# Output projection in borrowed PSUM banks, the last Q products one step earlier, snapshots at high priority and phi of Q in pairs, in a linear-attention block with a ReGLU MLP

## The chip, the cores and the metric

The kernel runs on one core of a Trainium2 chip. The metric is the device time of one execution in microseconds (us), the median of several runs. A profile is one execution recorded by the hardware profiler; its span is somewhat shorter than that execution's own time.

## The reference

Input is x of 2048 tokens by 1024, in bf16. The block computes h = x + attention(layernorm(x)) and then h + MLP(layernorm(h)):

```python
qkv = (x @ wqkv) split into q, k, v of 32 heads with 32 columns each
phi = lambda t: jnp.where(t > 0, t + 1, jnp.exp(t)) + 1e-6
pq, pk = phi(q), phi(k)
kv = jnp.einsum("bhsd,bhse->bhde", pk, v)
z = jnp.einsum("bhsd->bhd", pk)
num = jnp.einsum("bhqd,bhde->bhqe", pq, kv)
den = jnp.einsum("bhqd,bhd->bhq", pq, z)[..., None] + 1e-6
o = (num / den) @ wo
...
gate = h_ln @ W_gate          # kept where positive, 0 elsewhere
up = h_ln @ W_up
out = h + (gate * up) @ W_down  # W_gate, W_up: 1024 x 3584
```

## The kernel before

**Large products.** They are done by a scheme of seven block products in place of eight (Strassen's, in Winograd's form) over two by two blocks; the sums of operands are made on VectorE. The generator `strassen` (L144) runs one unit: seven products for two neighbouring column tiles v = 0 and 1, in six phases, each ended by a `yield`. Its PSUM tiles come from the pool `pspool`: two banks of tag A, two of tag E, one of tag D. A collects products 1, 6, 7 and 4 one upon the other; after each of the first three a snapshot of A is copied to SBUF by ScalarE (`snap`, L149; the copy is L153). D takes product 2; E takes products 5 and 3. `fin` makes a result out of a PSUM tile and a snapshot.

**Stages.** First layernorm of x, K and V and the products kv and z, token tile by token tile (up to about 124 us in the profile). Then Q: `q_unit(s, c)` makes Q transposed for the half s of the columns of tokens, in units of two column blocks c and c + 1. The two units of s = 0 run alone (124 to 148 us). The two units of s = 1, twelve phases in all, are dealt out over eight attention steps (`QSTEPS` = 8) in the list `rest`: one or two phases behind each step. Each result of Q goes through phi: `phi_begin` (L189) adds the snapshot, and `phi_end` (L197) does an exp on ScalarE (L199), then a min with an add (L200) and a max (L201) on VectorE. Before the change that is done for each 128 x 512 tile by itself.

**Attention steps.** `attn_stages(t)` (L495) has five stages for a tile of 128 tokens: `nd` (numerators and denominators: eight matmuls L509 in three pieces, each a PSUM tile of tag "ab"; ScalarE takes Ln and Exp of the denominators, L513 and L515; VectorE multiplies, L516), `oT` (a DMA transpose, L523), `x_in` (a load of x, L527), `wo_h` (the output projection: two PSUM tiles "attn", also of tag "ab", with eight matmuls each, L536; VectorE adds x and sums rows, L538; the sum of both is scaled in L546; then on ScalarE the layernorm's Square, Ln, Exp, scale and normalise, L548 to L552) and `hn_T` (a DMA transpose of the normalised tile, L555). `attn_step(step)` issues stage k of the tile that began LAG[k] steps earlier, with LAG = (0, 1, 1, 2, 4), so in step n stand nd of tile n, oT and x_in of tile n - 1, wo_h of tile n - 2 and hn_T of tile n - 4. Behind hn_T of the later tiles of a half, `left_sums` makes the operand sums for the MLP (L117 to L120). The pool "ab" has three PSUM banks. Tiles 0 to 7 are those of s = 0, tiles 8 to 15 those of s = 1.

**What comes after.** From step 8 on, four "early quads" of the MLP (units of `strassen` with `early_quad`, matmuls L693, results L702 to L708, written to DRAM) run beside the steps: the first phase of the first quad is issued ahead of step 8, the others from step 12 on in the list `flow`. Then all PSUM pools are closed, the pool `accs` takes their banks (tag A two buffers of two banks, X and Y one each), and the rest of the MLP runs (`quad`, matmuls L773; then the down projection, L934 and L1105) in an order written out by hand for TensorE, ScalarE and VectorE.

**What sets the order.** In the part up to there the order of the instructions on each engine is planned when the kernel is built: a planner (Tile) takes the instructions in the order in which the program lists them, which is their priority, draws ready ones of a lower priority forward where an engine would stand idle by its own costs, and gives out the tiles of a tag as they come free. `tc.high_priority()` puts what is issued in it ahead of the others. A block ahead of everything else (L378) runs 16 matmuls on zeros ("spin", L383) while the first data load; their PSUM tile has tag E.

Of the kernel before, what the change touches and what calls it, by code (L numbers as in the profile page):

```python
# [31 lines left out]
def block_kernel(ctx: ExitStack, tc: tile.TileContext, x, wqkv, wo, wg, wu, wd, out, H: int):  # L32
# [111 lines left out]
    def strassen(pool, work, mm, fin, sbufs=3):  # L144


        A, E, snaps = {}, {}, {}

        def snap(v, nm):  # L149
            if v == 0:  # L150
                snaps[nm] = work.tile([P, 2, NW], FP32, tag="snap", bufs=sbufs, name=nm)
            snaps[nm, v] = snaps[nm][:, v, :]
            nc.scalar.copy(out=snaps[nm, v], in_=A[v][:])  # L153

        def m2(v):
            d = pool.tile([P, NW], FP32, tag="D", bufs=1, name="Dq")
            mm(d, 2, v, True)
            fin(0, 0, v, d, snaps["m1", v])

        for v in range(2):  # L160
            A[v] = pool.tile([P, NW], FP32, tag="A", bufs=2, name="Aq")
            mm(A[v], 1, v, True)
            snap(v, "m1")
        yield
        m2(0)
        for v in range(2):
            mm(A[v], 6, v, False)
            snap(v, "u2")
        m2(1)
        yield  # L170
        for v in range(2):
            E[v] = pool.tile([P, NW], FP32, tag="E", bufs=2, name="Eq")
            mm(E[v], 5, v, True)
        yield
        for v in range(2):
            mm(A[v], 7, v, False)
            snap(v, "u3")
            fin(1, 1, v, E[v], snaps["u3", v])
        yield
        for v in range(2):  # L180
            mm(A[v], 4, v, False)
            fin(1, 0, v, A[v], None)
        yield
        for v in range(2):
            mm(E[v], 3, v, False)
            fin(0, 1, v, E[v], snaps["u2", v])
        yield
# [9 lines left out]
    def phi_end(dst, e):  # L197

        nc.scalar.activation(out=e, in_=dst, func=ACT.Exp, bias=negb[:, 0:1], scale=1.0)  # L199
        nc.vector.tensor_scalar(out=e, in0=e, scalar1=1.0, scalar2=PHI_EPS, op0=ALU.min, op1=ALU.add)  # L200
        nc.vector.tensor_tensor(out=dst, in0=dst, in1=e, op=ALU.max)  # L201
# [9 lines left out]
    with ExitStack() as actx:  # L211
# [166 lines left out]
        with tc.high_priority():  # L378
            zero = asmall.tile([P, NW], BF16, tag="zero", bufs=1, name="zero")
            nc.vector.memset(zero[:], 0.0)  # L380
            spin = pspool.tile([P, NW], FP32, tag="E", bufs=2, name="spin")
            for n in range(SPIN):
                nc.tensor.matmul(spin[:], lhsT=zero[:, 0:P], rhs=zero[:], start=True, stop=True)  # L383
            ln_T(atiles[0])
# [45 lines left out]
    def q_unit(s, c):  # L430

        left = left_ops(xT[s], xS[s])
        ready = {}

        def mm(ps, m, v, start):
            for kc in range(KH):
                nc.tensor.matmul(ps[:], lhsT=rq[m - 1][:, kc, (c + v) * P:(c + v + 1) * P],  # L437
                                 rhs=left[m - 1][:, kc, :], start=(start and kc == 0),
                                 stop=(kc == KH - 1), skip_group_check=True)

        def fin(i, j, v, ps, m):
            dst = pqT[:, j * KH + c + v, i * HS + s * SW:i * HS + (s + 1) * SW]
            phi_begin(dst, ps, m)
            e = qw[-1].tile([P, NW], BF16, tag="e", name="e")
            phi_end(dst, e[:])

        return strassen(pspool, qw[-1], mm, fin)

# [46 lines left out]
    def attn_stages(t):  # L495

        i, r = divmod(t * P, HS)
        s, r = divmod(r, SW)
        st = {}

        def nd():
            o_sb = bwork.tile([P, D], BF16, tag="o_sb", name="o_sb")
            st["o"] = o_sb
            held.append(o_sb)
            ov = o_sb[:].rearrange("p (k h e) -> p k h e", k=KC, h=HPC)
            for c0, n in pieces:
                ps = ndpool.tile([P, NW], FP32, tag="ab", name="nd")
                for c in range(c0, c0 + n):
                    nc.tensor.matmul(ps[:, (c - c0) * NDW:(c - c0 + 1) * NDW], lhsT=pqT[:, c, t * P:(t + 1) * P],  # L509
                                     rhs=kvz[:, c, :], start=True, stop=True)  # L510
                ndv = ps[:, 0:n * NDW].rearrange("p (k w) -> p k w", w=NDW)
                den = bsmall.tile([P, GPB, HPC], FP32, tag="den", name="den")
                nc.scalar.activation(out=den[:, 0:n], in_=ndv[:, :, P:NDW], func=ACT.Ln, bias=deps[:], scale=1.0)  # L513
                rd = bsmall.tile([P, GPB, HPC], FP32, tag="rd", name="rd")
                nc.scalar.activation(out=rd[:, 0:n], in_=den[:, 0:n], func=ACT.Exp, scale=-1.0)  # L515
                nc.vector.tensor_tensor(  # L516
                    out=ov[:, c0:c0 + n], in0=ndv[:, :, 0:P].rearrange("p k (h e) -> p k h e", h=HPC),
                    in1=rd[:, 0:n, :].unsqueeze(3).to_broadcast([P, n, HPC, Dh]), op=ALU.mult)

        def oT():  # L520
            oT = bwork.tile([P, D], BF16, tag="oT", bufs=XB, name="oT")
            st["oT"] = oT[:].rearrange("p (c t) -> p c t", c=KC)
            nc.sync.dma_start_transpose(out=st["oT"], in_=st["o"][:])  # L523

        def x_in():
            x_sb = bwork.tile([P, D], BF16, tag="x_res", bufs=XB, name="x_res")
            nc.sync.dma_start(out=x_sb[:], in_=xf[t * P:(t + 1) * P, :])  # L527
            st["x"] = x_sb

        def wo_h():  # L530
            h_sb = st["x"]
            tot = bsmall.tile([P, 2], FP32, tag="tot", name="tot")
            for j in range(2):
                ps = abpool.tile([P, NW], FP32, tag="ab", name="attn")
                for c in range(KC):
                    nc.tensor.matmul(ps[:], lhsT=st["oT"][:, c, :], rhs=wo_sb[:, c, j * NW:(j + 1) * NW],  # L536
                                     start=(c == 0), stop=(c == KC - 1))
                nc.vector.scalar_tensor_tensor(out=h_sb[:, j * NW:(j + 1) * NW], in0=ps[:], scalar=1.0,  # L538
                                               in1=h_sb[:, j * NW:(j + 1) * NW], op0=ALU.mult, op1=ALU.add,
                                               accum_out=tot[:, j:j + 1])  # L540
            nc.sync.dma_start(out=h_dram[i][s][:, r // P, :], in_=h_sb[:])
            st["hn"] = bwork.tile([P, D], BF16, tag="hn", bufs=HB, name="hn")

            sm = bsmall.tile([P, 6], FP32, tag="sm", name="sm")
            nmean, var, lnv, rstd, nmr = (sm[:, i:i + 1] for i in range(5))
            nc.vector.tensor_scalar(out=nmean, in0=tot[:, 0:1], scalar1=tot[:, 1:2], scalar2=-1.0 / D,  # L546
                                    op0=ALU.add, op1=ALU.mult)
            nc.scalar.activation(out=st["hn"][:], in_=h_sb[:], func=ACT.Square, bias=nmean, scale=1.0, accum_out=var)  # L548
            nc.scalar.activation(out=lnv, in_=var, func=ACT.Ln, bias=LN_EPS, scale=1.0 / D)
            nc.scalar.activation(out=rstd, in_=lnv, func=ACT.Exp, scale=-0.5)  # L550
            nc.scalar.activation(out=nmr, in_=nmean, func=ACT.Identity, scale=rstd)
            nc.scalar.activation(out=st["hn"][:], in_=h_sb[:], func=ACT.Identity, bias=nmr, scale=rstd)  # L552

        def hn_T():
            nc.sync.dma_start_transpose(out=hnT[s][i][:, :, r:r + P], in_=st["hn"][:])  # L555

        return nd, oT, x_in, wo_h, hn_T
# [7 lines left out]
    def attn_step(step):  # L565
        for k in range(len(LAG)):
            n = step - LAG[k]
            if n in begin_at:
                n = begin_at.index(n)
                stages[n][k]()  # L570
                if k == len(LAG) - 1 and n % STS >= NT:
                    left_sums(hnT[n // STS], hns[n // STS], slice(n % NT * P, (n % NT + 1) * P), nc.vector)

    rest = [p for s in range(1, NS) for c in range(0, KH, 2) for p in [q_unit(s, c)] * 6]
    for step in range(QSTEPS):
        attn_step(step)
        if step:
            for _ in range(-(-len(early_loads) // (QSTEPS - step))):
                early_loads.pop(0)(held[step][0:1, 0:1])
        for p in rest[step * len(rest) // QSTEPS:(step + 1) * len(rest) // QSTEPS]:  # L580
            next(p)
    q1ctx.close()
    xctx[1].close()
# [748 lines left out]
```

## Time and profile before

| | us |
|---|---|
| median of 3 runs | 748.55 |
| lowest and highest | 747.36, 749.38 |
| the profiled execution, its own time | 748.8 |
| its span in the profile | 747.0 |
| TensorE busy in the span | 725.9 |
| VectorE, ScalarE busy | 568.4, 324.6 |
| projection of tile 6 starts (step 8) | 204.97 |
| first matmul of the hand-ordered MLP (L773) starts | 297.49 |

How to read the profile: PE is TensorE's matmuls, PEld its weight loads, DVE is VectorE, ACT is ScalarE, POOL is GpSimd, SP the queue that issues most DMAs. A group is named by its line in the kernel, then engine, operation, what it writes and what it reads. A wait "PE attn L536 <- DVE o_sb L516: 2.4, 4, 0.9" says that TensorE stood idle ahead of instructions of L536 until an instruction of L516 on VectorE was over: 2.4 us in total, 4 times, at most 0.9. In a table of stretches each line has the stretch, its length, the busy time of each engine with the number of its instructions, the granted clock, the DMA share and GB/s.

### The profile page before, as it was taken

The page shows a single profiled execution, that of the slowest core. Times are in us where ns is not written, and L with a number is a line of the kernel's source. Part 1 is how long each engine was busy: PE and PEld are TensorE (multiplying, and loading weights), DVE is VectorE, ACT ScalarE, POOL GpSimd, SP SyncE. Part 2 cuts the span into 40 slices and gives each one's busy share as a digit, 9 for nine tenths or more (in the row PEclk, how much of TensorE's full clock was granted, in tenths as well). Part 3 has the DMA queues.
Part 4 walks back from the last instruction along what each step waited for, and adds up shares of the span by engine and source line. Part 5 has one row for each costly group of instructions (what it writes and reads, how often), then busy time and mean ns, then how long its engine had stood idle before and what let it go on. Part 6 is the DMA issues. An engine that isn't in the chain of part 4 may idle for free.

```text
span 747.0 us, 10654 instructions
## 1 busy us (share of the span) xinstructions
PE 725.9 (97%) x4020; PEld 382.2 (51%) x4020; DVE 568.4 (76%) x1023; ACT 324.6 (43%) x596; POOL 5.8 (1%) x44
## 2 busy tenths in 40 slices
PE   7999999999889999999999999999999999999997
PEld 3444555444344444444444444444444458888666
DVE  6997644777886767678777788877787469996797
ACT  4876554778767645344444344343435220000000
POOL 0000000000000000000000000000000000000000
PEclk9999999999999999999999999999999999999999
DMA  9766002069777525164837349476574399988822
GB/s 317 159 145 154 1 1 94 20 146 249 170 173 172 134 79 183 39 182 121 237 127 207 125 140 317 149 211 212 183 261 149 101 388 361 317 284 299 306 79 79
DMA packets 146580, 132.03 MB, mean 177 GB/s; under 512 B 50913, under 2 KB 128097, under 8 KB 146529
## 3 DMA queue, kind: packets, MB, share of 16 engines
q1 hardware_dynamic: 135392, 123.23, 54.4%
q10 hardware_dynamic: 11136, 8.13, 3.4%
q8 instruction: 31, 0.51, 0.3%
q14 instruction: 21, 0.16, 0.1%
HBM read 79.95 MB, written 39.85 MB: 160 GB/s over the span
## 4 chain that ended last, share of the span: by engine, by line
PE 79%; DVE 8%; ACT 5%; DMA 5%; issue 1%; SPq 0%; POOL 0%; DVEq 0%; ACTq 0%
PE accA L773 22%; PE accY L773 8%; PE accX L773 8%; PE accA L1105 8%; PE attn L536 5%; PE Aq L297 3%; PE accA L934 3%; PE accX L1105 3%; PE Aq L437 3%; PE accY L1105 2%; DMA hn<-hn 2%; PE Aq L693 2%; PE Eq L297 2%; PE accX L934 2%; PE accY L934 2%
## 5 line engine op out<-in xcount | busy, mean ns | idle before, releaser
L783 ACT ACTIVATE gu<-gu 128x512 bf16<-128x512 bf16 x72 | 45.4, 630 | 131.9 <-DVE gu L782 127.4
L778 ACT COPY snap<-accA 128x1024 f32<-128x1024 f32 x72 | 72.4, 1008 | 37.0 <-PE accA L773 36.9
L536 PE MATMUL attn<-wo_mem,oT 128*128 128x512 bf16 x256 | 57.8, 379 | 3.4 <-DVE o_sb L516 3.1
L773 PEld LDWEIGHTS <-tg 128*128 128x128 f16 x384 | 37.6, 98 | 45.3
L773 PEld LDWEIGHTS <-tu 128*128 128x128 f16 x384 | 37.6, 98 | 45.3
L782 DVE TENSOR_TENSOR gu<-accY,snap 128x1024 bf16<-128x1024 f32 x36 | 43.9, 1219 | 9.7 <-ACT snap L778 9.7
L153 ACT COPY u<-Aq 128x512 f32<-128x512 f32 x56 | 32.2, 581 | 43.9 <-PE Aq L297 20.3
L782 DVE TENSOR_TENSOR gu<-accX,snap 128x1024 bf16<-128x1024 f32 x36 | 43.9, 1219 | 7.2 <-PE accX L773 4.7
L773 PE MATMUL accA<-hn,tg 128*128 128x512 f16 (+1 forms) x192 | 49.3, 379 | 0.0
L773 PE MATMUL accA<-hn,tu 128*128 128x512 f16 (+1 forms) x192 | 49.3, 379 | 0.0
L1105 PEld LDWEIGHTS <-x 128*128 128x128 f16 (+1 forms) x448 | 43.8, 98 | 5.5
L773 PEld LDWEIGHTS <-wg 128*128 128x128 bf16 x288 | 28.2, 98 | 34.9 <-issue 1.1
L773 PEld LDWEIGHTS <-wu 128*128 128x128 bf16 x288 | 28.2, 98 | 34.0
L536 PEld LDWEIGHTS <-oT 128*128 128x128 bf16 x256 | 25.0, 97 | 35.0 <-issue 6.7
L786 DVE TENSOR_TENSOR hq<-gu 128x512 bf16<-128x512 bf16 x48 | 20.3, 423 | 14.3 <-ACT gu L783 14.2
L297 PEld LDWEIGHTS <-xT 128*128 128x128 bf16 (+1 forms) x192 | 18.6, 98 | 24.5 <-issue 3.2
L516 DVE TENSOR_TENSOR o_sb<-nd,rd 128x384 bf16<-128x384 f32 (+1 forms) x48 | 22.8, 507 | 8.6 <-ACT rd L515 7.5
L1105 PEld LDWEIGHTS <-xs 128*128 128x128 f16 x280 | 27.4, 98 | 3.2
L538 DVE SCALAR_TENSOR_TENSOR x_res<-attn,x_res 128x512 bf16<-128x512 f32 x32 | 22.0, 688 | 6.3 <-PE attn L536 6.2
L934 PEld LDWEIGHTS <-x 128*128 128x128 bf16 (+1 forms) x168 | 16.5, 98 | 19.6
L1111 DVE TENSOR_TENSOR snap<-accA,u 128x1024 f32<-128x1024 f32 x16 | 19.5, 1220 | 8.3 <-PE accA L1105 8.1
L773 PE MATMUL accA<-hn,wg 128*128 128x512 bf16 x96 | 24.6, 379 | 0.8 <-DVE gu L702 0.8
(232 smaller groups left out, 1415.0 us busy)
## 6 DMA issues: line engine op xcount, KB each, us to landing
x<-x_dram SPq DMA_DIRECT2D x17, 896.0 KB, 8.2
x_dram<-hq SPq DMA_DIRECT2D x28, 512.0 KB, 3.0
wg<-in_B_W_gate_dram SPq DMA_DIRECT2D x14, 512.0 KB, 5.2
wu<-in_B_W_up_dram SPq DMA_DIRECT2D x14, 512.0 KB, 7.4
wraw<-in_B_W_down_dram SPq DMA_DIRECT2D x14, 512.0 KB, 4.9
x_dram<-hq SPq DMA_DIRECT2D x28, 256.0 KB, 2.6
t_dram<-wt SPq DMA_DIRECT2D x28, 256.0 KB, 2.2
xd<-x_dram SPq DMA_DIRECT2D x6, 896.0 KB, 7.2
```

The costliest lines, as they stand in the source:

```text
L153: nc.scalar.copy(out=snaps[nm, v], in_=A[v][:])
L297: nc.tensor.matmul(ps[:], lhsT=left[m - 1][:, kc, r + v * P:r + (v + 1) * P], rhs=right[m - 1][:, kc, :], start=(start and kc == 0), stop= ...
L437: nc.tensor.matmul(ps[:], lhsT=rq[m - 1][:, kc, (c + v) * P:(c + v + 1) * P], rhs=left[m - 1][:, kc, :], start=(start and kc == 0), stop=( ...
L516: nc.vector.tensor_tensor(out=ov[:, c0:c0 + n], in0=ndv[:, :, 0:P].rearrange("p k (h e) -> p k h e", h=HPC), in1=rd[:, 0:n, :].unsqueeze(3 ...
L536: nc.tensor.matmul(ps[:], lhsT=st["oT"][:, c, :], rhs=wo_sb[:, c, j * NW:(j + 1) * NW], start=(c == 0), stop=(c == KC - 1))
L538: nc.vector.scalar_tensor_tensor(out=h_sb[:, j * NW:(j + 1) * NW], in0=ps[:], scalar=1.0, in1=h_sb[:, j * NW:(j + 1) * NW], op0=ALU.mult, ...
L773: nc.tensor.matmul(ps[:, v, :], lhsT=w[v][n - 1][:, kc, :], rhs=left[n - 1][:, kc, :], start=(t is not None and kc == 0), stop=(kc == KH - ...
L778: nc.scalar.copy(out=st[nm][:], in_=halves(st["A"]))
L782: add(out=g[:], in0=halves(st[nm]), in1=st[base][:], op=ALU.add)
L783: nc.scalar.activation(out=g[:, 0, :], in_=g[:, 0, :], func=ACT.Relu)
L934: nc.tensor.matmul(ps[:, t * NW:(t + 1) * NW], lhsT=x_tile(n, s, kh)[:, f, (t0 + t) * P:(t0 + t + 1) * P], rhs=w_tile(n, kh)[:, f, :], sta ...
L1105: nc.tensor.matmul(pv[:, tt, :], lhsT=left(m)[:, f, tt * P:(tt + 1) * P], rhs=right(m)[:, f, :], start=(t is not None and f == 0 and tt % ...
```

## The change

Four edits that hang together, and one small one. The output projection `wo_h` takes its two PSUM tiles from tag E of `pspool` in steps 8 to 11, which are the projections of tiles 6 to 9, and from "ab" in all other steps. In step 7 the phases of Q that are due (the last two) are issued ahead of the attention step, not behind it. Every snapshot copy is issued at high priority. Phi of Q puts both column blocks of a unit into one tile: `phi_begin` stays as it was for each, and `phi_end` runs once for 128 x 2 x 512 when the second is there. The spin tile takes tag A.

```diff
@@ strassen, snap @@
             snaps[nm, v] = snaps[nm][:, v, :]
-            nc.scalar.copy(out=snaps[nm, v], in_=A[v][:])
+            with tc.high_priority():
+                nc.scalar.copy(out=snaps[nm, v], in_=A[v][:])
@@ at the start of the K and V stage @@
-            spin = pspool.tile([P, NW], FP32, tag="E", bufs=2, name="spin")
+            spin = pspool.tile([P, NW], FP32, tag="A", bufs=2, name="spin")
@@ q_unit @@
         def fin(i, j, v, ps, m):
-            dst = pqT[:, j * KH + c + v, i * HS + s * SW:i * HS + (s + 1) * SW]
-            phi_begin(dst, ps, m)
-            e = qw[-1].tile([P, NW], BF16, tag="e", name="e")
-            phi_end(dst, e[:])
+            pair = pqT[:, j * KH + c:j * KH + c + 2, i * HS + s * SW:i * HS + (s + 1) * SW]
+            phi_begin(pair[:, v], ps, m)
+            if v == 1:
+                e = qw[-1].tile([P, 2, NW], BF16, tag="e", name="e")
+                phi_end(pair, e[:])
@@ attn_stages @@
-        def wo_h():
+        def wo_h(borrow):
...
             for j in range(2):
-                ps = abpool.tile([P, NW], FP32, tag="ab", name="attn")
+                if borrow:
+                    ps = pspool.tile([P, NW], FP32, tag="E", bufs=2, name="attn")
+                else:
+                    ps = abpool.tile([P, NW], FP32, tag="ab", name="attn")
@@ attn_step @@
-                stages[n][k]()
+                if k == 3:
+                    stages[n][k](QSTEPS <= step < STS + LAG[-1])
+                else:
+                    stages[n][k]()
@@ the eight steps beside Q @@
     for step in range(QSTEPS):
+        now = rest[step * len(rest) // QSTEPS:(step + 1) * len(rest) // QSTEPS]
+        if step == QSTEPS - 1:
+            while now:
+                next(now.pop(0))
         attn_step(step)
         if step:
             for _ in range(-(-len(early_loads) // (QSTEPS - step))):
                 early_loads.pop(0)(held[step][0:1, 0:1])
-        for p in rest[step * len(rest) // QSTEPS:(step + 1) * len(rest) // QSTEPS]:
+        for p in now:
             next(p)
```

## Prediction

> **What bounds the kernel now.** I read the page's engine table and its slices first, then a table of stretches, then TensorE's own waits in the stretches that lag, then the timelines of TensorE, ScalarE and VectorE there.
>
> ```profile
> PE 725.9 (97%) x4020; PEld 382.2 (51%) x4020; DVE 568.4 (76%) x1023; ACT 324.6 (43%) x596; POOL 5.8 (1%) x44
> PE   7999999999889999999999999999999999999997
> ```
>
> TensorE (PE) is busy 97% of a 747.0 us span, so only the moments when it stands still can be won. Slices 11 and 12 (about 187 to 224 us) are the only ones below nine tenths apart from the first and the last. The table of stretches (PE, weight loads, VectorE, ScalarE, GpSimd) sizes this:
>
> ```profile
> 148.00:198.90 50.90, 49.93 (x274) 23.88 (x273) 38.43 (x99) 40.81 (x113) 1.49 (x8) 1.00 0.81 189
> 198.90:231.50 32.60, 26.55 (x146) 12.63 (x145) 27.93 (x81) 22.96 (x66) 0.00 (x0) 1.00 0.69 162
> 231.50:297.50 66.00, 62.62 (x305) 28.70 (x304) 46.87 (x113) 39.47 (x90) 0.00 (x0) 1.00 0.52 144
> 300.00:350.00 50.00, 50.00 (x234) 22.66 (x232) 37.57 (x74) 21.21 (x30) 0.00 (x0) 1.00 0.35 107
> ```
>
> PE is idle 0.97 us in the attention steps that run beside the Q products, 32.60 - 26.55 = 6.05 us in the steps after them (step 8 on), and 66.00 - 62.62 = 3.38 us where attention runs beside the early MLP quads: 10.4 us together. From 300 us on it shows no idle at all until the last few us. So the MLP's hand-ordered part starts when this stage ends, and each microsecond of idle removed here should come off the time. PE's waits in the two stretches (198 to 232, then 232 to 298):
>
> ```profile
> PE attn L536 <- DVE o_sb L516: 2.4, 4, 0.9
> PE nd L509 <- DVE x_res L538: 1.9, 2, 1.3
> PE nd L509 <- DVE pq_mem L201: 1.8, 1, 1.8
> ...
> PE Aq L693 <- ACT m L153: 1.8, 1, 1.8
> PE accA L773 <- DVE gu L702: 0.8, 1, 0.8
> PE Aq L693 <- ACT u L153: 0.4, 1, 0.4
> ```
>
> Lines 1 and 2 are PSUM banks: L516 is the last reader of an nd bank, L538 that of an output-projection bank, and both kinds rotate through the three "ab" banks, five tiles a step. Line 3 is phi of Q, not ready when nd of step 8 wants it. Lines 4 and 6 are snapshots that leave late. Line 5 is the first MLP tile, waiting until an old E bank has been read. On the timelines, the output projections (L536) of steps 8 to 12 start at 204.97, 210.52, 215.85, 222.05 and 228.08 us: 23.11 us for four steps.
>
> [...] the second snapshot of a quad, whose matmuls had ended by 268.3 us sat behind a Square that began only at 270.06, with ScalarE idle for 2.03 us, and left at 271.21. [...] the trace has medians of 721 and 1148 (L199, Q and K). I use the trace's.
>
> **The change, part by part**, against the profiled execution's own 748.8 us (span 747.0, 1.8 around it; the median of the runs is 748.55, 0.25 less).
>
> **Borrowed banks.** Steps 8 to 11 write both projection tiles to the E banks. E's last user before is Q's last product (198.45, read by 201.2), the next is an early quad's product at 232.18, so they are free. No matmul is added. nd then has three "ab" banks for its three pieces, and the projection waits for its predecessor's L538 a step earlier. Removed: 2.37 + 1.87 = 4.24 us. What is late next? PE's own work in a step is 16 projection matmuls in 3.45 us (start to start of the next instruction) and 8 nd matmuls in 0.47: 3.92. ScalarE's is the chain Square, Ln, Exp, scale, normalise from 210.08 to 213.37, 3.29 us, and den and rd of three pieces, about 1.0: 4.3. VectorE's: two L538 (0.69 each), three L516 (about 1.3), the small sum and in most steps four half-tile sums at 0.34: some 4.4. So ScalarE and VectorE are longer than PE's bare step, and what hides this is other PE work: between 198.88 and 231.5 PE also ran about 5 us of early-quad matmuls, 1 us a step or more, giving 4.9 a step. With that cover I leave 0.3 us of stall in each of four steps: gain 3.0. If the cover is used up in the first two steps, the rest run at 4.4 to 4.9 and only about 1.5 is gained; the ceiling is 4.2.
>
> **Q products ahead.** The last two phases of Q (16 matmuls, 3.45 us; two Identity and four exps on ScalarE, made fewer below; the adds and phi on VectorE) go ahead of step 7. They issue no DMA. What they pass is nd of tile 7, the transposes and loads of step 7 on SP's queue, and the projection of tile 5 (PE 195.00). The weight loads tied to step 7 with their GpSimd holds stay behind the step. Q's last matmul thus ends about 195.5 instead of 198.9, and phi, which ended at 203.78, is ready around 200, while nd of step 8 isn't due before the projection of tile 5 ends at about 201. The 1.79 us wait goes. New: the projection of tile 5 still uses "ab" banks, and must wait for the nd of tile 7 right before it (Ln, Exp, L516: 1.5 to 2 us) with no Q matmuls between. The first early-quad products (1.73 us, their hn landed in time for 198.88) can stand there. I take 0.3 of new stall: gain 1.5; ends 0 (the wait just moves) and 1.8.
>
> **Snapshots first.** Same copies (0.58 us each), earlier in ScalarE's queue. Candidates: 1.82 and 0.39 here, 0.39 and 0.33 in the first K unit, 2.93 together. A snapshot put ahead of its data would hold Ln, Exp and Square behind it; the 1.15 us Square is what now stands in front. I take 2.2; the bounds are 2.9 and a loss (below, as a rival).
>
> **Phi pairwise.** Sixteen pairs. ScalarE: two exps issue 0.61 apart, 1.22; one of 1024 takes 1.06: 16 x 0.16 = 2.6 us of occupancy. VectorE: the K rows give 0.33 and 0.60 for the 1024 forms against 2 x 0.20 and 2 x 0.33: 16 x 0.13 = 2.1 us. Neither engine bounds before 198.9, so none of it counts directly; it pays for the room assumed above. The cost is latency: the last pair is ready about 0.44 + 0.13 + 0.27 = 0.8 us later. At nd of tile 0 (a 0.23 us wait on L201 now) this falls on PE, where Q products of the next half can be put in between: I take -0.4 (ends -0.9 and 0). At step 8 the earlier Q covers it.
>
> **The spin tile.** It moves from tag E to A, so tag A is the first one asked for in the pool, and I take it that banks are laid out in that order. The first accumulator of the MLP then lies over A banks, last read at 295.77, instead of E banks, read until 297.45; its second operand's bank is not needed until 1.73 us later. Gain 0.8, or 0 if the layout doesn't follow.
>
> Sum: 3.0 + 1.5 + 2.2 - 0.4 + 0.8 = 7.1. Every queue's order is planned anew, and the traced order already departs from program order (a second quad's product runs at 214.33); for fresh small waits in K, V and the quads I take off 1.3 (ends 0 and 3; existing ones there are 0.2 to 1.5 us apiece). Net 5.8: 748.8 - 5.8 = **743.0 us**. The stage's ceiling, all 10.4 idle and 0.7 in K, would give 737.7.
>
> **Rivals.** *ScalarE becomes the bound of steps 8 to 12.* It is busy 22.96 of 32.60 us now; at 4.3 us a step plus the 0.9 us that it now waits for nd in each (0.98, 0.93 and 0.97 ahead of L513), a step is 5.2 against 5.78: 2.3 saved. With spin 0.8 and snapshots 0.4, about 3.5 less 1.0 for planning: 746.3. For it: the chain of 3.29 us is serial. Against: den and rd can fill its gaps. *Nothing moves:* the planner already drew ready work forward, so Q's phases and snapshots land where they were, and the E tiles wait on oT instead: 748. Against: the waits name banks, and oT is issued some 9 us before its use (206.67 for 215.85). *Slower:* snapshots at the head of ScalarE's FIFO. From 148 to 297 us there are 36 of them (six in each of two Q units and four quads); if each stands 0.2 us before its matmuls end, with nd's Ln and the Square behind it, PE loses up to 7.2 us, against 4.9 of other gains less 1.3, so 3.6 are lost on balance: 752.4. It decides from 0.1 us a snapshot. Against: ScalarE has 10 us free there in 32.6, and a snapshot can only be placed after its matmuls.
>
> **How the numbers follow.** About 0.3%, 2.2 us, can be told from no change. Forecast (gain 3.5 to 8): 0.63. Nearly all idle gone (8 to 10.5): 0.06. ScalarE bound (1.5 to 3.5): 0.17, two thirds of it beyond 2.2. Nothing moves: 0.06. Slower: 0.08. So faster 0.80, same 0.12, slower 0.08. The range, 739.8 to 747.2, leaves out most of the slower case and some of the best and of "nothing": nearly 0.2.
>
> **What would show it.** Right: no wait of nd on L538 and none of attn on L516 in steps 8 to 11, their pitch at 4.4 to 5.2 us; no nd wait on L201 at step 8; no Aq wait on L153 over 0.5 us; the first accA with no gap; the first L773 matmul at about 291.7 us instead of 297.49. Wrong: that matmul within 2 us of 297.5, with waits on L515 or L552 in place of the banks'; or snapshots with long idle before them on ScalarE while den and Square are ready; or idle on PE after 300 us, where I assume none appears.

## The result and the profile after

The changed kernel takes 743.07 us (median of four runs, 742.23 to 745.54) against 748.43 for the kernel before beside it (747.36 to 749.38): a ratio of 0.9934, with the interval 0.9906 to 0.9963. The forecast was 743.0. The profiled execution of after took 742.45 us, with a span of 740.6. Of its page, the engine table and TensorE's slices; 53 of its matmul records are missing, so its 721.8 is too low:

```profile
PE 721.8 (97%) x3967; PEld 382.0 (52%) x4020; DVE 563.2 (76%) x991; ACT 322.0 (43%) x580; POOL 5.7 (1%) x44
PE   7999999999989999999999999999999999999997
```

Of the two weak slices one is left. A table of stretches cut at the same work in both kernels shows where the time went: from nd of tile 0 to the projection of tile 5, from there to that of tile 10, and on to the first accA matmul. First before, then after (columns: stretch, length, PE, weight loads, VectorE, ScalarE, GpSimd, clock, DMA share, GB/s):

```profile
147.93:195.00 47.07, 46.10 (x255) 22.18 (x254) 35.20 (x91) 37.19 (x107) 1.18 (x7) 1.00 0.83 188
195.00:228.08 33.08, 27.03 (x148) 12.85 (x147) 29.79 (x87) 23.50 (x64) 0.31 (x1) 1.00 0.67 159
228.08:297.49 69.41, 66.03 (x319) 30.25 (x319) 48.31 (x117) 42.62 (x99) 0.00 (x0) 1.00 0.53 148
```

```profile
146.24:195.38 49.14, 47.69 (x261) 23.20 (x264) 35.27 (x82) 38.39 (x95) 1.58 (x7) 1.00 0.86 182
195.38:222.09 26.71, 23.11 (x131) 11.37 (x133) 24.03 (x70) 21.39 (x70) 0.31 (x1) 1.00 0.85 198
222.09:291.11 69.02, 66.94 (x319) 30.64 (x324) 50.41 (x124) 41.07 (x94) 0.00 (x0) 1.00 0.56 145
```

The first part grew by 2.07 us, because the last Q products and the first quad's products now stand in it; the second lost 6.37, part of it that same work; the third lost 0.39. Together the stage is 149.56 before and 144.87 after: 4.69 us. Since the same matmuls are done (720 weight loads before, 721 after), that should be idle time. The first accA matmul starts 6.38 us earlier; the other 1.69 us are there before nd of tile 0 already (147.93 against 146.24), where x and the weights of Q land. Of the terms of the forecast only two snapshot waits lie there, 0.39 and 0.33 us in the first K unit, and they did not shrink (0.52 and 0.33 after). TensorE's waits in the stage after:

```profile
PE Eq L705 <- DVE hs L117: 2.0, 1, 2.0
PE Aq L438 <- ACT u L154: 1.1, 1, 1.1
PE nd L511 <- DVE o_sb L518: 1.0, 2, 0.8
PE Aq L705 <- ACT m L154: 0.7, 1, 0.7
PE Aq L705 <- ACT u L154: 0.6, 2, 0.3
PE attn L541 <- DVE o_sb L518: 0.4, 1, 0.4
PE attn L541 <- DMA oT<-o_sb: 0.3, 1, 0.3
```

The lines are shifted: L511 is nd, L518 its last reader, L541 the projection, L154 the snapshot, L438 Q's products, L705 the early quads'. No wait of nd on the projection's reader is left, none on phi, none of accA. New are 2.0 us for an operand sum (hs, L117), 1.1 us for a snapshot in the Q units, and 1.0 us of nd on o_sb, the reader of its own banks.

### The profile page after: what moved, and what is told of

Read it like the earlier page. It is cut to its first block, busy times and chain, and to the rows that moved or that the text cites. A ratio compares the mean times of both kernels' runs of the same rounds, so it can differ in the third digit from the quotient of the medians.

```text
span 740.6 us, 10570 instructions
## 1 busy us (share of the span) xinstructions
PE 721.8 (97%) x3967; PEld 382.0 (52%) x4020; DVE 563.2 (76%) x991; ACT 322.0 (43%) x580; POOL 5.7 (1%) x44
## 4 chain that ended last, share of the span: by engine, by line
PE 78%; DVE 8%; ACT 7%; DMA 5%; issue 2%; SPq 0%; DVEq 0%; POOL 0%; ACTq 0%
PE accA L785 22%; PE accX L785 8%; PE accY L785 8%; PE accA L1117 8%; PE Aq L298 3%; PE accA L946 3%; PE accX L1117 3%; PE Aq L438 3%; DMA hn<-hn 2%; PE accY L1117 2%; PE attn L541 2%; PE Aq L705 2%; PE Eq L298 2%; PE accY L946 2%; PE accX L946 2%
## 5 line engine op out<-in xcount | busy, mean ns | idle before, releaser
L541 PE MATMUL attn<-wo_mem,oT 128*128 128x512 bf16 x249 | 57.9, 379 | 1.2 <-DVE o_sb L518 0.4
L154 ACT COPY u<-Aq 128x512 f32<-128x512 f32 x56 | 32.4, 582 | 37.3 <-PE Aq L298 19.3
L541 PEld LDWEIGHTS <-oT 128*128 128x128 bf16 x256 | 24.6, 98 | 30.8 <-issue 2.9
L518 DVE TENSOR_TENSOR o_sb<-nd,rd 128x384 bf16<-128x384 f32 (+1 forms) x48 | 22.8, 507 | 4.5 <-ACT rd L517 4.4
L785 PE MATMUL accA<-hn,wu 128*128 128x512 bf16 x96 | 24.6, 379 | 0.0
```

The source lines that it names most:

```text
L518: nc.vector.tensor_tensor(out=ov[:, c0:c0 + n], in0=ndv[:, :, 0:P].rearrange("p k (h e) -> p k h e", h=HPC), in1=rd[:, 0:n, :].unsqueeze(3 ...
L785: nc.tensor.matmul(ps[:, v, :], lhsT=w[v][n - 1][:, kc, :], rhs=left[n - 1][:, kc, :], start=(t is not None and kc == 0), stop=(kc == KH - ...
```

## The experiments

Each time stands beside runs of the kernel before on the same chip: 748.92 us for the first four, 748.73 for the next four, 748.87 for the last four. "Clock" is the granted TensorE clock as a mean over the span.

### Each large part alone

The borrowed banks alone, on the kernel before:

```diff
-                ps = abpool.tile([P, NW], FP32, tag="ab", name="attn")
+                if borrow:
+                    ps = pspool.tile([P, NW], FP32, tag="E", bufs=2, name="attn")
+                else:
+                    ps = abpool.tile([P, NW], FP32, tag="ab", name="attn")
```

> The kernel before with the borrowed banks alone. Theory A (the record's sum): the bank waits of steps 8 to 11 go (4.24 us) and about 3.0 us come off, 745.4. Theory B (read off the two traces): the banks' wait only hides the arrival of tile 7's normalised rows, which the first quad needs; that wait shows up as one of about 2 us on the sums of L117, and with the wait of 1.8 us on phi of Q still there about 1 to 2 us come off, 746.5 to 747.5. Theory C: the planner's new order decides, and the gain isn't tied to the waits: bank waits stay, or the stage is longer in places that the edit doesn't touch.

Measured: 749.09 us, ratio 0.9995 (0.9978 to 1.0012): no gain in the median. All bank waits of steps 8 to 11 were gone, and yet the stage took 151.42 us. In VectorE's timeline of this kernel one operand sum stands for 3.65 us ahead of its data, with the scale of the layernorm (L549) and three o_sb behind it:

```profile
213.30 0.08 DVE L541 DVE_READ_ACCUMULATOR x_res<-attn,x_res 128x1 f32 x1
217.03 0.43 DVE L117 TENSOR_TENSOR hs<-hn 128x512 f16<-128x512 bf16 x1 [3.65 <-DMA hn<-hn]
217.37 0.21 DVE L549 TENSOR_SCALAR sm<-tot 128x1 f32<-128x1 f32 x1
...
218.50 1.34 DVE L516 TENSOR_TENSOR o_sb<-nd,rd 128x384 bf16<-128x384 f32 x3
```

On TensorE's timeline the consequence is a wait of 2.56 us for o_sb, and then something else:

```profile
212.93 3.61 PE L539 MATMUL attn<-wo_mem,oT 128*128 128x512 bf16 x16
219.10 1.07 PE L509 MATMUL nd<-kvz,pq_mem 128*128 128x132 bf16 x8 [2.56 <-DVE o_sb L516]
221.45 1.01 PE L699 MATMUL Eq<-hs,tg 128*128 128x512 f16 x2 [1.28 <-DVE hs L117]
222.26 1.91 PE L699 MATMUL Aq<-hs,tg 128*128 128x512 f16 x4
```

Four matmuls of 512 columns take 1.91 us here, where after has 1.02 for the same four. The stretches around it give the reason in the clock column (1.00, 0.50, 0.80):

```profile
218.50:219.50 1.00, 0.34 (x3) 0.21 (x3) 1.00 (x4) 0.91 (x5) 0.00 (x0) 1.00 1.28 247
...
221.50:226.50 5.00, 5.00 (x12) 1.68 (x12) 3.56 (x10) 3.91 (x10) 0.00 (x0) 0.50 1.06 243
226.50:227.50 1.00, 1.00 (x5) 0.44 (x4) 0.00 (x0) 0.51 (x1) 0.00 (x0) 0.80 0.05 13
```

TensorE is fully busy from 221.5 to 226.5 at half clock: 2.5 us of work are lost there, after 3.84 us of standing still. A second such spell, from 271.3 to 274.7, follows a wait of 2.32 us for a snapshot. The runs of this one program bear it out: 744.79 us at a mean clock of 0.999, 745.80 and 746.32 at 0.997, 749.21 at 0.992, 749.91 at 0.992. From 0.999 to 0.992 is 0.7% of some 747 us, 5.2 us, and the first and last of these differ by 5.1. All twelve runs lie near one line, with 0.76 us for each 0.001 of clock. At a clock of 0.999 or above the kernel before took 747.27 to 748.53 us on this chip (7 of 39 runs), so at the full clock the banks are worth about 3 us, though only one of their own runs reached it. They did win their time, and the clock took it back in most runs.

The Q products ahead of step 7, alone:

```diff
+        if step == QSTEPS - 1:
+            while now:
+                next(now.pop(0))
         attn_step(step)
```

> The kernel before with the last two phases of Q ahead of step 7, alone. Theory A: the 1.8 us wait of nd on phi goes and 0.3 comes new: 1.5 us off, 746.9. Theory B: the wait goes but the bank waits behind it take its place, as the step's pitch is set by them: 0 to 1 us off, 747.5 to 748.5. Theory C: no wait on phi, yet others elsewhere, time either side of 748.4.

Measured: 749.05 us, ratio 1.0003 (0.9993 to 1.0014), the lower end that the forecast gave, where the wait just moves. At full clock it is even slower: 748.42 to 749.42 us in four runs, against 747.27 to 748.08 in four of the kernel before. Why it loses there was not found. Phi's 1.79 us are gone, but the projection of tile 5, on the "ab" banks, now stands right behind nd of tile 7 (TensorE's timeline), and the bank waits stay:

```profile
199.13 3.61 PE L536 MATMUL attn<-wo_mem,oT 128*128 128x512 bf16 x16 [1.87 <-DVE o_sb L516]
204.61 3.61 PE L536 MATMUL attn<-wo_mem,oT 128*128 128x512 bf16 x16 [0.39 <-DVE o_sb L516]
```

Both together:

> The kernel before with both the borrowed banks and the early Q products. Theory A: 3.0 and 1.5 add up to 4.5 off, 743.9. Theory B: both feed the same chain (tile 7's layernorm and transpose), so that together they give about 3 us, 745.4, with a wait of about 2 us on the sums of L117 ahead of the first quad's second product. Theory C: no regular relation to the two alone.

Measured: 744.42 us, ratio 0.9945 (0.9929 to 0.9961): 4.5 us, what the forecast gave for the two (3.0 + 1.5), though the median of each alone shows nothing. Three of its four runs are at full clock and none below 0.998, against a mean of 0.997 for the kernel before and 0.994 for the banks alone, so part of the 4.5 us is clock.

The snapshots alone:

```diff
-            nc.scalar.copy(out=snaps[nm, v], in_=A[v][:])
+            with tc.high_priority():
+                nc.scalar.copy(out=snaps[nm, v], in_=A[v][:])
```

> The kernel before with the snapshots at high priority, alone. Theory A: the Aq waits on L153 shrink from 2.9 us to 0.7, 2.2 us off, 746.2. Theory B: as in the trace after, only the longest of them shrinks (1.8 to 0.7) and others of 0.3 to 0.5 stay, since the snapshot is placed by the planner's clock and the chip's differs: about 1 us off, 747.4. Slower rival: snapshots hold ScalarE's queue, 749 or more.

Measured: 749.29 us, ratio 1.0008 (0.9999 to 1.0018): no gain. ScalarE's timeline shows two snapshots (L154) and a Square (L549) ahead of phi's last exp (L200), which ends at 200.93:

```profile
198.04 0.56 ACT L154 COPY m<-Aq 128x512 f32<-128x512 f32 x1
198.51 1.15 ACT L549 ACTIVATE hn<-x_res,sm 128x1024 bf16<-128x1024 bf16 x1
...
199.65 0.57 ACT L154 COPY m<-Aq 128x512 f32<-128x512 f32 x1
...
200.22 0.71 ACT L200 ACTIVATE e<-pq_mem,negb 128x512 bf16<-128x512 bf16 x1
```

```profile
203.30 0.29 PE L510 MATMUL nd<-kvz,pq_mem 128*128 128x132 bf16 x1 [3.06 <-DVE pq_mem L202]
203.76 2.72 PE L537 MATMUL attn<-wo_mem,oT 128*128 128x512 bf16 x6 [0.17 <-DVE o_sb L517]
```

So nd (second fence, TensorE) waits 3.06 us for phi, before 1.79, and the projection behind it runs at half clock: six matmuls in 2.72 us at a clock of 0.50, where the kernel before has 1.46 for six at 189.75 us. In the kernel before, the second of these snapshots came behind the exp, so the priority cost the exp some 0.6 us: the slower rival of the forecast, with another victim than nd's Ln. That is not the whole of it. The min of phi (L201), next in line after the exp, stood on VectorE behind an operand sum that waited for its transposed tile, as with the banks alone:

```profile
201.94 0.43 DVE L117 TENSOR_TENSOR hs<-hn 128x512 f16<-128x512 bf16 x1 [0.96 <-DMA hn<-hn]
202.29 0.28 DVE L201 TENSOR_SCALAR e<-e 128x512 bf16<-128x512 bf16 x1
```

And the snapshot wait of 1.8 us near 272 us was still there, at 1.95. The likely reason is that high priority orders what the planner sees as ready, and that by its costs the Square was ready first. That is inferred from the order on ScalarE; no trace shows the planner's list.

### One part less at a time

In each of these, one part of the change is undone in the kernel after, by the reverse of its hunk.

> The changed kernel with the projection back in the three ab banks in all steps. Theory A: the bank waits return, 3.0 us lost of 5.4: 746.1. Theory B: banks' waits of 4 us return but the wait for tile 7's sums (2.0 us) and those of nd on L518 (1.0) go: 1 to 2 us lost, 744.1 to 745.1. Theory C: no loss.

> The changed kernel with the last two phases of Q behind step 7 again. Theory A: 1.5 us lost, 744.6, with nd of step 8 waiting about 2 us for phi (longer by the pair's 0.8). Theory B: that wait comes back, but falls into time that the first quad's sums would take anyway, so 0.5 to 1.5 lost: 743.6 to 744.6. Theory C: no loss.

> The changed kernel with snapshots at their plain priority. Theory A: 2.2 us lost, 745.3. Theory B: about 1 us lost, 744.1, all of it in the early quads. Theory C: no loss or a gain.

> The changed kernel with phi of Q tile by tile again. Theory A: 0.4 us gained by the shorter latency, 742.7. Theory B: phi's 2.6 us of ScalarE come back in the steps beside Q, where ScalarE is busy 39 of 50 us, and delay the layernorm: 0.5 to 1 us lost, 743.6 to 744.1. Theory C: within 0.3 us.

> The changed kernel with the spin tile back in tag E. If the pool's layout follows the first use of its tags, the first accumulator of the MLP lies over E banks again, the wait of accA on the MLP's gu product (0.78 us before) is back, and the time is 743.1 + 0.8 = 743.9. If the layout doesn't follow, 743.1 and no such wait. All the kernels so far with the spin in E showed 0.78 there and all with it in A showed none, so the first is expected.

| undone | us | ratio to before, interval | more than after's 743.07 |
|---|---|---|---|
| borrowed banks | 745.71 | 0.9965 (0.9955 to 0.9975) | 2.6 |
| Q ahead | 744.41 | 0.9953 (0.9933 to 0.9973) | 1.3 |
| snapshots | 743.47 | 0.9944 (0.9921 to 0.9966) | 0.4 |
| phi pairs | 745.79 | 0.9961 (0.9949 to 0.9972) | 2.7 |
| spin tile | 743.68 | 0.9940 (0.9919 to 0.9961) | 0.6 |

After's own interval is 4 us wide, so only the first and fourth rows stand out, and their intervals still touch after's. The rows come from more than one chip; by the ratios the last column would read 2.3, 1.4, 0.7, 2.0 and 0.4. Runs at a clock of 0.999 or above separate the first row: 745.29 to 746.26 us without the banks (eight runs), against 742.23 and 742.45 for after, about 3 us as in the banks alone. What the traces add is firmer. Without the borrowed banks the bank waits are back (5.7 us, ten times) at full clock. With the spin tile back in tag E one wait is back as it was:

```profile
291.63 1.02 PE L785 MATMUL accA<-hn,wg 128*128 128x512 bf16 x4 [0.78 <-DVE gu L714]
```

It stood in every kernel of this study with the spin in E and in none with it in A.

Without the phi pairs the trace has no longer wait on phi. It has one of 3.06 us on an oT transpose, and a half-clock spell from 216.4 to 223.2 us (TensorE's timeline):

```profile
213.88 0.51 PE L510 MATMUL nd<-kvz,pq_mem 128*128 128x132 bf16 x6
217.46 2.32 PE L540 MATMUL attn<-wo_mem,oT 128*128 128x512 bf16 x5 [3.06 <-DMA oT<-o_sb]
```

Its 16 runs go from 743.81 us at full clock to 747.63 at 0.995. The two at full clock (743.81 and 744.12) lie 1.6 us above after's two (742.23 and 742.45), so about 1 us of the 2.7 is clock again. Why that transpose falls due late in this plan, whether for the 1.8 us that ScalarE has more to do (323.8 against 322.0 busy) or because another order came out, was not separated.

### Taking the block off VectorE's queue

The sharp test of the account for the banks: the same borrowed banks on the kernel before, and the operand sums of three tiles in four issued one step later, when their transposes have landed.

```diff
+                    late.append(n)
+                    for m in late[:] if n % STS == STS - 1 else late[:-1]:
+                        late.remove(m)
+                        left_sums(hnT[m // STS], ...)
-                    left_sums(hnT[n // STS], ...)
```

> The kernel before with borrowed banks, and the operand sums of the MLP (L117) of tiles 4 to 6 and 12 to 14 issued one step later; no work is added or left out. If the gain of the banks was lost because one sum stood at the head of VectorE's queue for 3.65 us waiting for its transposed tile (o_sb and the scale behind it, PE starved at 218 to 222 us, and the granted clock then 0.5 for the next stretch), that block goes, the clock stays at 0.998 or above, and the banks alone are worth about 3 us: 745 to 746. If borrowing is worth nothing for another reason (the steps bound by ScalarE, or Q's phi), the time stays at 748.5 to 749.5 with new waits on other lines.

Measured: 743.76 us (742.84 to 744.42), ratio 0.9933 (0.9919 to 0.9947), clock 0.998 to 1.000. The same program as the banks alone but for the order of the sums is 5.3 us faster. In VectorE's timeline this sum no longer waits, and o_sb comes when it is wanted:

```profile
215.84 0.68 DVE L541 SCALAR_TENSOR_TENSOR x_res<-attn,x_res 128x512 bf16<-128x512 f32 x1
216.44 0.08 DVE L541 DVE_READ_ACCUMULATOR x_res<-attn,x_res 128x1 f32 x1
216.44 0.42 DVE L117 TENSOR_TENSOR hs<-hn 128x512 f16<-128x512 bf16 x1
216.92 0.69 DVE L541 SCALAR_TENSOR_TENSOR x_res<-attn,x_res 128x512 bf16<-128x512 f32 x1
```

TensorE still waits 2.56 us, at 218 us, for the sum of the last tile of the half, which is issued at once as before, but no spell at half clock follows (clock 1.00 from 214 to 234 us). Of the 5.3 us, the runs at the best clock (744.79 at 0.999 against 742.84 at 1.000, with 0.76 us for each 0.001) give about 1.2 to the waits themselves and the rest to the clock. What the late sums would do without the banks wasn't run: in the kernel before, too, three of four L117 sat idle for 2.6 us in that stretch.

The same on top of the change:

> The changed kernel with the same later sums. The two waits of nd on o_sb (1.0 us in all) lie behind sums in VectorE's queue: they go if that is their cause, and the time is 742.0 to 742.5. The 2.0 us wait of the first quad's product on its sum stays or grows by up to 0.3, because the sum of tile 7 is still issued at once. If the sums hide nothing, 743 within 0.5; if they pile up ahead of the quad's first product, 744 to 745.

Measured: 744.54 us, ratio 0.9943 (0.9929 to 0.9956): 1.5 us more than after, not less. The sums no longer block, but o_sb was late for another reason, in ScalarE's queue: the Square (L553) writes a buffer that an hn transpose is still reading. That transpose was issued at 211.13, 1.2 us after its tile was ready (209.95), behind an oT and a load on SP's queue, and these transposes take 4.4 us from issue to landing there (median of four). ScalarE's line, then TensorE's:

```profile
216.33 1.15 ACT L553 ACTIVATE hn<-x_res,sm 128x1024 bf16<-128x1024 bf16 x1 [1.64 <-DMA hn<-hn]
```

```profile
218.18 0.28 PE L511 MATMUL nd<-kvz,pq_mem 128*128 128x132 bf16 x2 [1.58 <-DVE o_sb L518]
218.30 0.81 PE L710 MATMUL Dq<-hn,wg 128*128 128x512 bf16 x3
221.19 1.44 PE L710 MATMUL Eq<-hs,tg 128*128 128x512 f16 x3 [2.09 <-DVE hs L117]
222.43 4.86 PE L541 MATMUL attn<-wo_mem,oT 128*128 128x512 bf16 x12
```

Two waits close together, 1.58 and 2.09 us, and the clock is 0.50 from 219.9 to 226.7: twelve matmuls take 4.86 us.

Last, the hn transpose issued first in each step as well:

```diff
-        for k in range(len(LAG)):
+        for k in (4, 0, 1, 2, 3):
```

> As the run before, and in each attention step the transpose of the normalised tile (hn) is issued first, ahead of that step's other transposes and loads on SP's queue. In the changed kernel tile 7 was normalised at 213.7 us but its transpose was issued only at 215.62, 1.9 us later, and the first quad's product then waited 2.0 us for the sum. If SP's order is the cause, that wait falls below 0.5 and the time is 740.5 to 741.5. If the transposes then collide, or the projection's own transpose (oT) becomes late in turn, new waits of attn on oT appear and the time is 742 to 744.

Measured: 741.55 us (741.31 to 741.87), ratio 0.9904 (0.9891 to 0.9918). It is the fastest of all; its four runs lie below the lowest of after (742.23), though the two intervals still overlap a little. The expectation was wrong about the way: the wait for the first quad's sum fell only from 2.00 to 1.76 us, since that transpose still left 2.1 us after its data (214.72 against 212.64), and an oT wait of 1.22 appeared. What went is the Square's wait (its transpose left 0.7 us after its data, and no Square waits for one between 203 and 219 us), the 0.76 us of nd behind it, and 0.8 us of the snapshot wait in the Q units; a wait of nd of 0.90 us at 203 is new. The stage is 143.87 us, 1.00 shorter than after, with no half-clock spell (mean clock 0.999).

## Why the prediction was right, and where it was not

The time was right: 743.0 predicted, 743.07 measured. The sum behind it was right in part, and that it came out this close is luck, as the terms show. The waits of the stage can be put against them. The two profiles have 9.88 us of waits before and 6.09 after (those over 0.2 us):

| term | predicted gain | waits before, after | gain in waits |
|---|---|---|---|
| borrowed banks | 3.0 | 4.87, 1.69 | 3.2 |
| Q ahead, and phi pairs | 1.5 - 0.4 | 2.02, 0 | 2.0 |
| snapshots | 2.2 | 2.21, 2.40 | -0.2 |
| spin tile | 0.8 | 0.78, 0 | 0.8 |
| fresh waits | -1.3 | 0, 2.00 | -2.0 |
| sum | 5.8 | 9.88, 6.09 | 3.8 |

**Banks: right in size by the runs, but not where the forecast put it.** The waits that the forecast named are gone. The projections of steps 9, 10 and 11 start at 203.80, 208.12 and 213.34 us, 4.3 and 5.2 apart, as foreseen; the next comes 8.75 later, with the sum's 2.00 us and early-quad products in it. So in this execution the four steps did not get shorter: 23.11 us before and 23.2 after (198.9 to 222.09), for nearly the same work and with 3.3 us of waits in each. Tile 7's sum took the place of the banks there, and the forecast, which asked what is late next, did not name it; what the stage gained lies ahead of step 8's projection (phi's 1.79 us and the 0.90 us behind it). The size of 3.0 us is read from the runs at full clock, with the banks alone and with the banks undone in the whole.

**Q ahead: right in company only.** Its end of 0 came true alone; undone in the whole it costs 1.3 us, which the noise does not set apart from nothing. The forecast had seen the reason, that the projection of tile 5 would wait for nd of tile 7, and thought that early-quad products would stand there. In after they do (193.65 to 195.38) and that wait is gone; alone it was 1.87 us.

**Snapshots: wrong, the step that failed.** The forecast said "Candidates: 1.82 and 0.39 here" and took 2.2 of 2.93. Of the pair here 0.73 and 0.34 stayed, 0.23 joined them, and 1.10 is new at 186 us, where a snapshot stands behind a normalise and two Ln on ScalarE. That last wait comes with the priority: it is there in all eight kernels that have it (0.26 to 1.32 us) and in none of the six that don't. Without the priority the kernel after has only 0.25 us of snapshot waits in the stage, which is 0.8 us shorter (144.08), and alone on the kernel before the priority makes 2.90 us of them out of 2.21. So the edit added what it was meant to remove; the fall from 1.82 to 0.73 is not its merit either. The forecast named the planner, which orders by its own times, and still priced the edit as if the queue were ordered by what happens on the chip. Undone in the whole, it costs 0.4 us, within the noise.

**Phi pairs: the wrong sign, as far as the runs tell.** Predicted -0.4; undone, the kernel is 2.7 us slower, 1.6 at full clock. The latency that the forecast feared isn't there: the 0.23 us wait at nd of tile 0 went away. Between the two kernels that differ in this part alone, ScalarE is busy 1.8 us less with the pairs (2.6 worked out) and VectorE 4.1 less (567.3 to 563.2, where 2.1 was worked out).

**Spin: right**, by mechanism and size.

**Fresh waits: right as a kind, low in size**, 2.0 for the sum alone. The other 0.9 us of the stage's 4.69 are not in the list, and gaps too short for it can't be all of them (0.5 us before: 10.40 idle, 9.88 listed); they stay open. The 1.69 us ahead of the stage are no term of the forecast. The first transposes of x start 0.75 us earlier in this execution (9.07 against 9.82), and the banks alone, which change nothing there, had 1.43 of the 1.69. But some 0.7 us seem to come with the priority, by a way that was not foreseen: the product that waits at 72 us in after starts 62.9 to 63.3 us behind those transposes in the eight kernels with the priority, 63.4 to 64.1 in the six without. Why was not tested. So the total of this execution rests on errors that offset each other: 2.4 us too much for the snapshots and 0.7 too little for new waits, against 1.1 too little for phi, Q ahead and the banks, 0.9 unaccounted for and 1.7 from a place that was not in the sum.

**The assumption that terms add was wrong.** Alone, the median of each of the three large parts shows no gain; two of them together are worth 4.5. Q ahead alone removes one of two waits in a row, so that the other is left to end last. The snapshots alone gain nothing at full clock either (747.08 to 748.10 us in four runs at 0.999, in the range of the kernel before). For the banks it is the clock, of which the forecast said nothing. In the profiled executions some plans lost time a second time, at half clock behind their waits: the banks alone had two half-clock spells (220.1 to 226.9 and 271.3 to 274.7 us), the snapshots one (202.3 to 209.1), Q ahead one (216.5 to 219.9), the kernel without phi pairs one (216.4 to 223.2), the late sums on top of the change one (219.9 to 226.7), before and after none. So the time of the rival "nothing moves" came true for each large part alone, by another mechanism, and for the whole not at all.

## What to carry to other kernels

Idle time of TensorE could not be summed over the trace and traded piece by piece here (4.5 us for two parts together, none in the median of each alone): ask of each plan where its longest cluster of waits lies, and read the clock in the stretches behind it (with the banks alone it was 0.50 for 6.8 us). Where one instruction that waits for a transfer holds up others of its engine (an operand sum for 3.65 us, three o_sb behind it), move it back before buying more buffers; here, with borrowed banks, sums issued one step later brought as much as the rest of the change did. And don't price a priority from what the trace shows to be late: here a planner stood between the two, and the waits grew.

## What was not expected of the hardware

Up to the last few microseconds, every stretch that was read in these traces has a granted clock of 1.00 or 0.50, with values between (0.96 or 0.62 in the two stretches of 0.5 us at the ends of one spell) only where it switches. A spell in mid-kernel lasted about 3.4 us twice and 6.8 us four times. The table has them as read from stretches of 0.5 us, with TensorE's waits of 0.6 us or more that end between 3 us ahead of a spell and its end:

| kernel | clock at 0.50 from, to | waits of TensorE |
|---|---|---|
| banks alone | 220.1, 226.9 | 2.56, 1.28 |
| banks alone | 271.3, 274.7 | 2.32 |
| Q ahead alone | 216.5, 219.9 | 1.28, 0.65 |
| snapshots alone | 202.3, 209.1 | 3.06 |
| after without phi pairs | 216.4, 223.2 | 3.06 |
| after with late sums | 219.9, 226.7 | 1.58, 2.09 |

What sets a spell off was not shown. The length of a wait does not sort them: 1.28 and 0.65 us close together are in the list, but after without Q ahead has 2.12 and 1.06 us close together, near 219, and after itself 0.76 and 2.00, and both stay at a mean clock of 1.000. The banks alone and the banks with late sums each have a wait of 2.56 us near 218. Their stretches before and from 218 us on, the banks alone first:

```profile
214.00:218.00 4.00, 2.54 (x12) 1.08 (x11) 0.97 (x4) 0.77 (x4) 0.00 (x0) 1.00 1.01 171
218.00:222.00 4.00, 1.49 (x10) 0.83 (x10) 4.00 (x13) 3.84 (x13) 0.00 (x0) 0.76 0.72 164
```

```profile
214.00:218.00 4.00, 4.00 (x25) 1.95 (x24) 3.94 (x14) 3.84 (x13) 0.00 (x0) 1.00 0.89 149
218.00:222.00 4.00, 1.44 (x7) 0.68 (x7) 2.67 (x9) 2.72 (x12) 0.00 (x0) 1.00 0.94 251
```

TensorE is busy for 1.49 and 1.44 us in the second stretches, and only the banks alone have a spell there; they had stood still for 1.46 us of the first one too. Runs of one kernel differ as well: after's are at a mean clock of 1.000 twice and of 0.998 twice (742.23 and 742.45, 743.68 and 745.54 us). Only one execution of each kernel was traced, so what the slower two met was not seen.
